# A new hand-written order for the first batch, and the seventh quad's rearrangement moved from GpSimd to VectorE

## The chip, the core and the metric

The kernel runs on one core of a Trainium2 chip. The core has a matrix engine (TensorE, in the profile PE for matmuls and PEld for the loading of their weights), VectorE (DVE), ScalarE (ACT), GpSimd (POOL) and SyncE (SP); 16 DMA engines move data between the chip's main memory and the core's on-chip memory. TensorE writes into PSUM, a small memory of eight banks, from which ScalarE and VectorE read. The metric is the device time in microseconds (us), taken as a median of several runs; lower is better.

## The reference

Attention with a squared ReLU in place of a softmax, and behind it a two-layer network over all heads of a token:

```
scores = (q @ k.T) / sqrt(64)              # per batch and head
attn   = max(scores, 0) ** 2 / 448
x      = (attn @ v), heads side by side    # 3584 x 768
h      = x @ w_in                          # 768 -> 2048
g      = max(h, 0) + alpha * min(h, 0)
out    = g @ w_out                         # 2048 -> 768, float32
```

There are 8 batches, 12 heads, 448 positions and a head width of 64. q, k, v and both weights arrive as float32; the kernel computes in bf16 and sums in float32.

## The kernel before, in words

**Quads and chunks.** Four heads make a quad, three quads a batch, so there are 24 quads. A quad's q and k come as one tile each (`raw`, three buffers per name), v as another (`vraw`, seven buffers). The 448 positions are cut into seven chunks.

**Turning.** Scores need q and k with the head width on the partitions (`T`, four buffers). Quads 0 to 4 are turned by TensorE (`turn_pe`, L149): 28 transposes into PSUM, and copies to `T` by VectorE or ScalarE at L159. From quad 5 on, one engine rearranges the rows into `perm` (L164) and a transposing DMA on SP's queue writes `T` (`turn_dma`, L167).

**Scores.** For each chunk `sc` issues four matmuls (L182) into a pair of PSUM banks, then a Relu by ScalarE (L191) or VectorE (L193) into `rl` (seven buffers). `sq` later squares it, on VectorE (L201) or ScalarE (L199), into `at` (twelve buffers). `late` is the list of chunks that wait for their square; `sq(k)` takes the first k of it.

**A@V.** `attnv` (L204) multiplies a quad's seven squared chunks with v: 28 matmuls (L211) into one pair of banks, which go to `xT`, one half by ScalarE (L221) and one by VectorE (L222); quad 0 alone is copied whole by ScalarE (L219).

**The network.** For the first layer `f1` computes one of 16 slices of 128 columns for a batch: six matmuls (L245), a scaled Relu by ScalarE (L253), and a multiply-add by VectorE (L254). The six matmuls take two from each quad of the batch, so part of a slice can be done before all quads are there: `some_early` does the first four of a slice and holds a PSUM bank for it. `f2` is the second layer, 16 matmuls a tile (L270), a copy by ScalarE (L272) and output DMAs on SP (L278). Columns 0 to 255 of the output use `w_out[0]`, the rest `w_out[1]`.

**Order.** The schedule is manual: each engine executes its instructions in the order in which the program emits them. Loads with a cast are issued from GpSimd's queue, also in order. PSUM banks go to the caller that comes next, always the bank or pair that was taken longest ago. So the order of the lines L286 to L340, the opening for batch 0, fixes four queues at once. Quad 0's q and k are loaded as float32 from SP's and ScalarE's queues and cast on the chip (L138 to L140); a tail of k comes through GpSimd.

**Quad 6.** L382 lets GpSimd rearrange its rows; L394 sends the transposing DMA after the second-layer tile `f2(0, 2, 0)`. The one-element copy to `landed` (L395) makes GpSimd's queue wait until that DMA has landed; behind it lie the last three pieces of `w_out[1]`, q and k of quad 9, and v of quads 6 and 7 (L396 to L399).

Of the kernel before, what the change touches and what calls it, by code (L numbers as in the profile page):

```python
# [16 lines left out]
NJ = 7  # L17
# [3 lines left out]
def kernel(  # L21
# [10 lines left out]
    nc = tc.nc  # L32
    B, H, S, D = q.shape
# [29 lines left out]
    landed = singles.tile([1, 1], BF16)  # L63
# [11 lines left out]
    def take_pair():  # L75
        lo = min((0, 2, 4, 6), key=lambda i: (max(taken[i], taken[i + 1]), i))
        take(lo, 2)
        return psum[:, lo:lo + 2]
# [7 lines left out]
    def take_bank():  # L86
        i = min(range(8), key=lambda i: (taken[i], i))
        take(i, 1)
        return psum[:, i]


    raw, vraw = {}, {}

    def load_qk(n, names="qk"):
        b, g = divmod(n, NG)
        for name in names:
            src = q if name == "q" else k
            t = raw_pool.tile([128, 2, NJ, D], BF16, tag=name, name=f"{name}raw")
            flat = src[b].rearrange("(m two) (pp j) d -> (two pp) m (j d)", two=2, j=NJ)
            nc.gpsimd.dma_start(out=t.rearrange("p m j d -> p m (j d)"), in_=flat[:, 2 * g:2 * g + 2])  # L100
            raw[(n, name)] = t

    def load_v(n):
        b, g = divmod(n, NG)
        t = v_pool.tile([128, 2, NJ, D], BF16, tag="v", name="vraw")
        flat = v[b].rearrange("(m two) (pp j) d -> (two pp) m (j d)", two=2, j=NJ)
        nc.gpsimd.dma_start(out=t.rearrange("p m j d -> p m (j d)"), in_=flat[:, 2 * g:2 * g + 2])  # L107
        vraw[n] = t
# [4 lines left out]
    def load_w_in(i):  # L113
        lo, hi = 512 * i, 512 * i + 512
        for hf in range(2):
            for e in range(2):
                nc.gpsimd.dma_start(out=w_in_sb[64 * hf:64 * hf + 64, :, e, lo:hi],  # L117
                                    in_=w_in_v[hf, e, :, :, lo:hi])

    def load_w_out(h, lo=0, hi=KF, step=4):  # L120
        for lo in range(lo, hi, step):
            nc.gpsimd.dma_start(out=w_out_sb[h][:, lo:lo + step], in_=w_out_v[:, lo:lo + step, COLS[h][0]:COLS[h][1]])

    FIRST = 4
    first, flat0 = {}, {}
# [9 lines left out]
    warm = psum[:, 7, :128]  # L135
    for _ in range(36):
        nc.tensor.matmul(warm, ident, ident, start=True, stop=True)
    for name, lo, hi, copy in (("q", 0, 4, nc.vector.tensor_copy), ("q", 4, NJ, nc.scalar.copy),  # L138
                               ("k", 0, 2, nc.vector.tensor_copy), ("k", 2, FIRST, nc.scalar.copy)):
        copy(raw[(0, name)][:, :, lo:hi].rearrange("p m j d -> p m (j d)"), first[name][:, :, D * lo:D * hi])  # L140
    load_qk(1)
    load_v(0)
    load_qk(2)
# [3 lines left out]
    T = {}  # L147

    def turn_pe(n, parts=(("q", 0, NJ, "D"), ("k", 0, NJ, "D"))):  # L149
        if n not in T:  # L150
            T[n] = T_pool.tile([128, 2, NJ, 128], BF16, tag="T", name="T")
        for name, lo, hi, eng in parts:
            ps = take_bank().bitcast(BF16)
            for j in range(lo, hi):
                for s in range(2):
                    nc.tensor.transpose(ps[64 * s:64 * s + 64, 128 * j:128 * j + 128], raw[(n, name)][:, s, j], ident)  # L156
            dst = T[n][:, "qk".index(name), lo:hi].rearrange("p j c -> p (j c)")
            copy = nc.vector.tensor_copy if eng == "D" else nc.scalar.copy
            copy(dst, ps[:, 128 * lo:128 * hi])  # L159

    def rearrange_rows(n, eng):
        p = perm_pool.tile([128, 2, NJ, 2, D], BF16, tag="perm", name="perm")
        for i, name in enumerate("qk"):
            eng.tensor_copy(p[:, i], raw.pop((n, name)).rearrange("p s j d -> p j s d"))  # L164
        return p

    def turn_dma(n, p=None):  # L167
        p = p or rearrange_rows(n, nc.vector)
        t = T_pool.tile([128, 2, NJ, 128], BF16, tag="T", name="T")
        nc.sync.dma_start_transpose(out=t.rearrange("p a j c -> p (a j) c"),  # L170
                                    in_=p.rearrange("p a j s d -> p (a j s d)"))
        T[n] = t
# [23 lines left out]
    def square(n, j, rl, eng="D"):  # L196
        a = at_pool.tile([128, 2, S], BF16, tag="at", name="at")
        if eng == "A":
            nc.scalar.activation(a, rl, ACTF.Square)  # L199
        else:  # L200
            nc.vector.tensor_tensor(a, rl, rl, ALU.mult)  # L201
        att[(n, j)] = a

    def attnv(n):  # L204
        ps = take_pair()
        vv = vraw.pop(n)
        for j in range(NJ):
            a = att.pop((n, j))
            for r in range(2):
                for s in range(2):  # L210
                    nc.tensor.matmul(ps[64 * s:64 * s + 64, r, :S],  # L211
                                     vv[64 * r:64 * r + 64, s, j, :],
                                     a[64 * r:64 * r + 64, s],
                                     start=(j == 0), stop=(j == NJ - 1))
        b, g = divmod(n, NG)
        if g == 0:
            xT[b] = xT_pool.tile([128, NG, 2, S], BF16, tag="xT", name="xT")
        if n == 0:
            nc.scalar.activation(xT[b][:, g], ps[:, :, :S], ACTF.Copy, scale=out_scale)  # L219
            return  # L220
        nc.scalar.activation(xT[b][:, g, 0], ps[:, 0, :S], ACTF.Copy, scale=out_scale)  # L221
        nc.vector.tensor_scalar(xT[b][:, g, 1], ps[:, 1, :S], out_scale, None, ALU.mult)  # L222

    late = []

    def sc(chunks):

        for n, j, eng in chunks:
            late.append((n, j, relu(score_mm(n, j), eng)))

    def sq(k=99, eng="D"):
        for g in late[:k]:
            square(*g, eng)
        del late[:k]
# [48 lines left out]
    def ch(n, lo, hi, p=pat):  # L283
        return [(n, j, p[j]) for j in range(lo, hi)]

    load_w_in(0)  # L286
    load_v(2)
    load_w_in(1)
    turn_pe(0, (("q", 0, 4, "D"), ("q", 4, NJ, "A"), ("k", 0, 2, "D"), ("k", 2, FIRST, "D")))
    sc(ch(0, 0, 3))  # L290
    turn_pe(0, (("k", FIRST, NJ, "D"),))
    sc(ch(0, 3, 4))
    sq(3)
    load_qk(3)
    sc(ch(0, 4, 6))
    turn_pe(1)
    sc(ch(0, 6, 7))
    sq(4)
    load_w_in(2)
    load_w_in(3)  # L300
    sc(ch(1, 0, 3, "AAA"))
    attnv(0)
    load_qk(4)
    sq(2)
    sc(ch(1, 3, 4))
    turn_pe(2)
    sq(1)
    sc([(1, 4, "D"), (1, 5, "A"), (1, 6, "A")])
    sq(2)
    load_w_out(0, 0, 8)  # L310
    load_qk(5)
    load_v(3)
    load_w_out(0, 8)
    early = {}
    todo = []

    def some_early(count):
        for ff, km in todo[:count]:
            if ff not in early:
                early[ff] = hold()  # L320
            f1_mm(psum[:, early[ff], :S], 0, ff, (km,))
        del todo[:count]

    sc(ch(2, 0, 3, "AAA"))
    sq(3)
    attnv(1)
    load_v(4)
    load_v(5)
    todo = [(ff, km) for ff in range(4) for km in range(4)]
    sc(ch(2, 3, 5, "AAAAAAA"))  # L330
    sq(2)
    some_early(4)
    sc(ch(2, 5, 7, "AAAAADA"))
    some_early(8)
    square(*late.pop(-2), "A")
    sq()
    attnv(2)
    nc.vector.tensor_scalar(beta_sb, alpha_sb, -1.0, 1.0, ALU.mult, ALU.add)
    some_early(4)
    for ff in range(4):  # L340
        f1_mm(psum[:, early[ff], :S], 0, ff, range(4, KM))
        f1_out(psum[:, early[ff], :S], 0, ff)
# [14 lines left out]
            turn_dma(n)  # L357
        load(n + 2)

    turn_pe(3)  # L360
    f1s(0, 4, 6)
    sc(ch(3, 0, 3))
    f1s(0, 6, 8)
# [15 lines left out]
    load_qk(6)  # L379
    load_qk(7)  # L380
    load_qk(8)
    rows6 = rearrange_rows(6, nc.gpsimd)  # L382
    load_w_out(1, 0, 4)
    f2(0, 0, 0)
    sq()
# [5 lines left out]
    sq()  # L391
    f2(0, 1, 0)
    f2(0, 2, 0)
    turn_dma(6, rows6)  # L394
    nc.gpsimd.tensor_copy(landed, T[6][:1, 0, 0, :1])  # L395
    load_w_out(1, 4)  # L396
    load_qk(9)
    load_v(6)
    load_v(7)  # L399
    sc(ch(5, 0, 3))  # L400
    sq(1)
    attnv(4)
# [20 lines left out]
    for ff in range(5):  # L423
        early.append(hold())
        f1_mm(psum[:, early[ff], :S], 1, ff, range(4))
        if ff == 1:
            sc(ch(5, 5, 7))
            sq(1)
            sq(1, "A")
        if ff == 3:  # L430
            attnv(5)
    for ff in range(KF):
        if ff < 5:
            f1_mm(psum[:, early[ff], :S], 1, ff, range(4, KM))
            f1_out(psum[:, early[ff], :S], 1, ff)
            take(early[ff], 1)
        else:
            f1(1, ff)
        if ff in (1, 10):
            turn_dma(7 + ff // 9)  # L440
        if ff == 10:
            nc.gpsimd.tensor_copy(landed, T[8][:1, 0, 0, :1])
            load_v(8)
            load_v(9)
            load(10)
# [21 lines left out]
    for b in range(2, B):  # L467
# [15 lines left out]
        for i, u in enumerate(units):  # L483
            if i in at and not last:
                g = at[i]
# [37 lines left out]
```

## Time and profile before

| what | value |
|---|---|
| median of 4 runs | 386.14 us (386.07 to 386.58) |
| the profiled execution's own time | 386.15 us |
| its span in the profile | 384.2 us |
| TensorE busy | 374.8 us, 3179 matmuls |
| VectorE busy | 265.6 us |
| ScalarE busy | 206.6 us |
| granted TensorE clock | full speed in every slice of the span |
| DMA engines | mean busy share 0.8 or more in each of the first twelve of forty slices |

The span runs from the first to the last instruction; about 2 us of the profiled time lie around it. A line of the timeline reads: start, time from the first instruction's start to the last one's end, engine, line of the code, operation, what is written and read, how many instructions are merged; in brackets the idle time ahead of them and who ended it. Instructions of one engine overlap a little, so the pace of a series is the distance between two starts, and is shorter than one instruction's own time.

### The profile page before, as it was taken

The page shows a single profiled execution, that of the slowest core. Times are in us where ns is not written, and L with a number is a line of the kernel's source. Part 1 is how long each engine was busy: PE and PEld are TensorE (multiplying, and loading weights), DVE is VectorE, ACT ScalarE, POOL GpSimd, SP SyncE. Part 2 cuts the span into 40 slices and gives each one's busy share as a digit, 9 for nine tenths or more (in the row PEclk, how much of TensorE's full clock was granted, in tenths as well). Part 3 has the DMA queues.
Part 4 walks back from the last instruction along what each step waited for, and adds up shares of the span by engine and source line. Part 5 has one row for each costly group of instructions (what it writes and reads, how often), then busy time and mean ns, then how long its engine had stood idle before and what let it go on. Part 6 is the DMA issues. An engine that isn't in the chain of part 4 may idle for free.

```text
span 384.2 us, 7843 instructions
## 1 busy us (share of the span) xinstructions
PE 374.8 (98%) x3179; PEld 205.7 (54%) x3200; DVE 265.6 (69%) x420; ACT 206.6 (54%) x331; POOL 70.1 (18%) x106
## 2 busy tenths in 40 slices
PE   7799999999999999999999999999999999999996
PEld 6444565555544455545465555544556445645554
DVE  4987987777657988688656887779855788526300
ACT  5978687445643654465444656547544475434321
POOL 8557070507302202022200222020000000000000
PEclk9999999999999999999999999999999999999999
DMA  9999989999993766687292872946035300120023
GB/s 161 190 202 202 189 125 196 171 175 207 220 220 61 109 116 109 109 134 119 49 165 60 135 122 51 166 77 119 15 85 88 77 0 15 44 68 2 14 68 85
DMA packets 73284, 43.42 MB, mean 113 GB/s; under 512 B 40352, under 2 KB 69792, under 8 KB 73248
## 3 DMA queue, kind: packets, MB, share of 16 engines
q0 software_dynamic: 26864, 22.45, 39.5%
q1 hardware_dynamic: 45952, 20.07, 26.7%
q8 instruction: 25, 0.41, 0.4%
q10 hardware_dynamic: 432, 0.39, 0.3%
q14 instruction: 11, 0.09, 0.1%
HBM read 45.62 MB, written 11.01 MB: 147 GB/s over the span
## 4 chain that ended last, share of the span: by engine, by line
PE 94%; DVE 3%; DMA 1%; issue 0%; ACT 0%; ACTq 0%
PE psum L245 38%; PE psum L270 38%; PE psum L182 9%; PE psum L211 8%; DVE at L201 2%; DMA qfirst<-in_q_dram 1%; PE psum L156 1%; DVE T L159 1%; DVE rl L193 1%; ACT osb L272 0%; DVE xT L222 0%; DVE qraw L140 0%; ACTq L278 0%; ACT T L159 0%
## 5 line engine op out<-in xcount | busy, mean ns | idle before, releaser
L270 PE MATMUL psum<-w_out,gT 128*128 128x256 bf16 (+3 forms) x891 | 149.9, 322 | 1.1
L245 PE MATMUL psum<-xT,w_in_sb 128*128 128x448 bf16 x768 | 150.1, 353 | 0.1
L270 PEld LDWEIGHTS <-gT 128*128 128x128 bf16 x912 | 86.7, 98 | 64.2 <-issue 8.2
L245 PEld LDWEIGHTS <-w_in_sb 128*128 128x128 bf16 x768 | 73.5, 98 | 73.2 <-issue 6.2
L254 DVE SCALAR_TENSOR_TENSOR gT<-neg,beta_sb,psum 128x448 bf16<-128x448 f32 x128 | 83.6, 678 | 35.4 <-ACT neg L253 35.3
L253 ACT ACTIVATE neg<-psum 128x448 f32<-128x448 f32 x128 | 69.2, 546 | 61.2 <-PE psum L245 59.4
L191 ACT ACTIVATE rl<-psum 128x896 bf16<-128x896 f32 x113 | 97.9, 931 | 1.7 <-PE psum L182 1.7
L201 DVE TENSOR_TENSOR at<-rl 128x896 bf16<-128x896 bf16 x164 | 92.1, 621 | 0.0
L193 DVE TENSOR_SCALAR rl<-psum 128x896 bf16<-128x896 f32 x55 | 59.7, 1086 | 40.3 <-PE psum L182 40.1
L272 ACT COPY osb<-psum 128x256 f32<-128x256 f32 (+3 forms) x57 | 26.9, 473 | 104.7 <-PE psum L270 99.0
L182 PE MATMUL psum<-T 64*64 64x448 bf16 x672 | 44.9, 356 | 3.0 <-DVE T L159 1.1
L100 POOL DMA_DIRECT2D qraw<-in_q_dram x23 | 16.6, 724 | 137.5 <-DVE perm L164 135.5
L211 PE MATMUL psum<-at,vraw 64*64 64x448 bf16 x672 | 36.7, 350 | 0.3 <-DVE at L201 0.2
L182 PEld LDWEIGHTS <-T 64*64 64x64 bf16 x672 | 16.7, 106 | 21.4 <-issue 13.1
L211 PEld LDWEIGHTS <-vraw 64*64 64x64 bf16 x672 | 21.1, 106 | 12.6 <-issue 2.5
L222 DVE TENSOR_SCALAR xT<-psum 128x448 bf16<-128x448 f32 x23 | 14.4, 624 | 14.4 <-PE psum L211 10.3
L107 POOL DMA_DIRECT2D vraw<-in_v_dram x24 | 17.5, 732 | 2.9 <-PE psum L182 1.0
L100 POOL DMA_DIRECT2D kraw<-in_k_dram x23 | 16.7, 727 | 2.5 <-DVE at L201 0.8
L221 ACT ACTIVATE xT<-psum 128x448 bf16<-128x448 f32 x23 | 12.6, 550 | 2.6 <-PE psum L211 2.6
L117 POOL DMA_DIRECT2D w_in_sb<-in_moe_w_in_dram x16 | 10.0, 632 | 6.3 <-DMA vraw<-in_v_dram 1.9
L164 DVE COPY perm<-kraw 128x896 bf16<-128x896 bf16 x18 | 11.0, 611 | 0.1
L164 DVE COPY perm<-qraw 128x896 bf16<-128x896 bf16 x18 | 11.0, 614 | 0.0
(29 smaller groups left out, 43.0 us busy)
## 6 DMA issues: line engine op xcount, KB each, us to landing
out_dram<-osb SPq DMA_DIRECT2D x54, 128.0 KB, 2.4
vraw<-in_v_dram POOLq DMA_DIRECT2D x24, 224.0 KB, 8.0
qraw<-in_q_dram POOLq DMA_DIRECT2D x23, 224.0 KB, 5.4
kraw<-in_k_dram POOLq DMA_DIRECT2D x23, 224.0 KB, 7.3
out_dram<-osb SPq DMA_DIRECT2D x56, 64.0 KB, 2.2
w_in_sb<-in_moe_w_in_dram POOLq DMA_DIRECT2D x16, 192.0 KB, 8.5
w_out<-in_moe_w_out_dram POOLq DMA_DIRECT2D x4, 512.0 KB, 9.2
w_out<-in_moe_w_out_dram POOLq DMA_DIRECT2D x4, 256.0 KB, 8.7
```

Source lines behind the costliest of these rows:

```text
L100: nc.gpsimd.dma_start(out=t.rearrange("p m j d -> p m (j d)"), in_=flat[:, 2 * g:2 * g + 2])
L164: eng.tensor_copy(p[:, i], raw.pop((n, name)).rearrange("p s j d -> p j s d"))
L182: nc.tensor.matmul(ps[64 * c:64 * c + 64, r, :S], t[64 * r:64 * r + 64, 1, j, 64 * c:64 * c + 64], t[64 * r:64 * r + 64, 0, :, 64 * c:64 * ...
L191: nc.scalar.activation(rl, ps[:, :, :S], ACTF.Relu)
L193: nc.vector.tensor_scalar(rl, ps[:, :, :S], 0.0, None, ALU.max)
L201: nc.vector.tensor_tensor(a, rl, rl, ALU.mult)
L211: nc.tensor.matmul(ps[64 * s:64 * s + 64, r, :S], vv[64 * r:64 * r + 64, s, j, :], a[64 * r:64 * r + 64, s], start=(j == 0), stop=(j == NJ ...
L245: nc.tensor.matmul(ps, w_in_sb[:, km // 2, km % 2, bass.ts(ff, 128)], xT[b][:, km // 2, km % 2, :], start=(km == 0), stop=(km == KM - 1))
L253: nc.scalar.activation(neg, ps, ACTF.Relu, scale=-1.0)
L254: nc.vector.scalar_tensor_tensor(gT[b // 2][:, ff, (b % 2) * S:(b % 2) * S + S], neg, beta_sb[:, ff:ff + 1], ps, ALU.mult, ALU.add)
L270: nc.tensor.matmul(ps, gT[sb][:, ff, bass.ts(c, 128)], w_out_sb[h][:, ff, lo:hi], start=(ff == 0), stop=(ff == KF - 1))
L272: nc.scalar.copy(o[:, lo:hi], ps)
```

## The change

- Quad 0: the casts are cut into six pieces (`cast0`), q on both engines and k on ScalarE alone; the turning is cut into nine pieces with a PSUM bank each.
- The order of batch 0 is written out anew: which chunk's Relu, which square, which copy comes when on which engine. `sq_of` squares a named chunk. The first two A@V come after the third quad's second chunk, and the 16 early matmuls of the first layer are issued as 11 and 5, all ahead of A@V of quad 2.
- Quad 0's A@V result is copied in halves by two engines, like the others'.
- In GpSimd's queue q and k of quad 3 come ahead of the second piece of `w_in`, and q and k of quad 4 ahead of its fourth.
- Quad 3 is turned ahead of the end of the first four slices, not behind them.
- Quad 6 is rearranged by VectorE inside `turn_dma(6)`, which now comes behind A@V of quad 5; the `landed` copy and the loads that were behind it move along.

```diff
-    for name, lo, hi, copy in (("q", 0, 4, nc.vector.tensor_copy), ("q", 4, NJ, nc.scalar.copy),
-                               ("k", 0, 2, nc.vector.tensor_copy), ("k", 2, FIRST, nc.scalar.copy)):
-        copy(raw[(0, name)][:, :, lo:hi].rearrange("p m j d -> p m (j d)"), first[name][:, :, D * lo:D * hi])
...
-        if n == 0:
+        if eng == "A":
             nc.scalar.activation(xT[b][:, g], ps[:, :, :S], ACTF.Copy, scale=out_scale)
...
+    def sq_of(n, j, eng):
+        for g in [g for g in late if g[:2] == (n, j)]:
+            square(*g, eng)
+            late.remove(g)
+
+    def cast0(name, lo, hi, eng):
+        copy = nc.vector.tensor_copy if eng == "D" else nc.scalar.copy
+        copy(raw[(0, name)][:, :, lo:hi].rearrange("p m j d -> p m (j d)"), first[name][:, :, D * lo:D * hi])
+
+    load_w_in(0)
+    load_v(2)
+    cast0("q", 4, 6, "A")
+    cast0("q", 0, 2, "D")
+    cast0("q", 6, 7, "A")
+    cast0("q", 2, 4, "D")
+    cast0("k", 0, 2, "A")
+    cast0("k", 2, 4, "A")
+    turn_pe(0, (("q", 0, 2, "D"),))
+    turn_pe(0, (("q", 4, 6, "A"),))
+    turn_pe(0, (("q", 2, 4, "D"),))
+    turn_pe(0, (("q", 6, 7, "A"),))
+    turn_pe(0, (("k", 0, 1, "D"),))
+    turn_pe(0, (("k", 1, 2, "A"),))
+    turn_pe(0, (("k", 3, 4, "A"),))
+    turn_pe(0, (("k", 2, 3, "A"),))
+    sc([(0, 0, "A")])
+    sc([(0, 1, "D")])
+    turn_pe(0, (("k", 4, 7, "D"),))
+    load_qk(3)
+    load_w_in(1)
+    load_w_in(2)
+    sq_of(0, 0, "D")
+    sc([(0, 2, "A")])
+    sc([(0, 3, "A")])
+    sq_of(0, 1, "D")
+    turn_pe(1, (("q", 0, 7, "D"),))
+    sc([(0, 4, "A")])
+    sc([(0, 5, "A")])
+    turn_pe(1, (("k", 0, 7, "D"),))
+    load_qk(4)
+    load_w_in(3)
+    sq_of(0, 2, "D")
+    sq_of(0, 5, "D")
+    sc([(0, 6, "A")])
+    sq_of(0, 4, "D")
+    sq_of(0, 6, "D")
+    sc([(1, 0, "A")])
+    sq_of(0, 3, "D")
+    sc([(1, 1, "A")])
+    sc([(1, 2, "D")])
+    sc([(1, 3, "A")])
+    sc([(1, 4, "A")])
+    sq_of(1, 0, "D")
+    turn_pe(2, (("k", 0, 5, "D"),))
+    turn_pe(2, (("q", 0, 7, "D"),))
+    sq_of(1, 2, "D")
+    sq_of(1, 4, "D")
+    turn_pe(2, (("k", 5, 7, "A"),))
...
+    sc([(1, 5, "A")])
+    sc([(1, 6, "A")])
+    sc([(2, 0, "A")])
+    sc([(2, 1, "A")])
+    sq_of(1, 1, "D")
+    sq_of(1, 5, "D")
+    sq_of(1, 3, "D")
+    sq_of(1, 6, "D")
+    attnv(0, "AD")
+    sc([(2, 2, "A")])
+    attnv(1, "AD")
+    sc([(2, 3, "A")])
+    sc([(2, 4, "D")])
+    sq_of(2, 0, "A")
+    some_early(11)
+    sq_of(2, 4, "A")
+    sc([(2, 5, "A")])
+    sq_of(2, 1, "D")
+    sq_of(2, 3, "D")
+    sq_of(2, 2, "D")
+    sc([(2, 6, "D")])
+    sq_of(2, 5, "A")
+    some_early(5)
+    sq_of(2, 6, "D")
     nc.vector.tensor_scalar(beta_sb, alpha_sb, -1.0, 1.0, ALU.mult, ALU.add)
-    some_early(4)
+    attnv(2, "AD")
+    some_early(0)
+    turn_pe(3, (("q", 0, 7, "D"),))
+    turn_pe(3, (("k", 0, 7, "D"),))
     for ff in range(4):
         f1_mm(psum[:, early[ff], :S], 0, ff, range(4, KM))
...
-    turn_pe(3)
     f1s(0, 4, 6)
...
-    rows6 = rearrange_rows(6, nc.gpsimd)
     load_w_out(1, 0, 4)
...
     f2(0, 2, 0)
-    turn_dma(6, rows6)
-    nc.gpsimd.tensor_copy(landed, T[6][:1, 0, 0, :1])
-    load_w_out(1, 4)
-    load_qk(9)
-    load_v(6)
-    load_v(7)
     sc(ch(5, 0, 3))
...
         if ff == 3:
             attnv(5)
+            turn_dma(6)
+            nc.gpsimd.tensor_copy(landed, T[6][:1, 0, 0, :1])
+            load_w_out(1, 4)
+            load_qk(9)
+            load_v(6)
+            load_v(7)
```

## The prediction, made before the changed kernel was built or run

> **What bounds the kernel now.** First the page's busy times and the chain that ended last:
>
> ```profile
> PE 374.8 (98%) x3179; PEld 205.7 (54%) x3200; DVE 265.6 (69%) x420; ACT 206.6 (54%) x331; POOL 70.1 (18%) x106
> ...
> PE 94%; DVE 3%; DMA 1%; issue 0%; ACT 0%; ACTq 0%
> ```
>
> TensorE sets the end. The change takes no matmul away, so it can only give back time in which TensorE waits. The stages (after each stage's length: PE, PEld, DVE, ACT, POOL busy, with counts) show where:
>
> ```profile
> 5.45:20.15 14.70, 11.48 (x217) 6.57 (x217) 13.78 (x27) 13.82 (x19) 9.08 (x15) 1.00 1.24 189
> 20.15:28.05 7.90, 7.90 (x92) 3.93 (x88) 6.31 (x12) 6.08 (x10) 4.79 (x8) 1.00 1.25 203
> 28.05:384.20 356.15, 351.42 (x2843) 191.39 (x2860) 244.92 (x382) 184.85 (x301) 51.51 (x74) 1.00 0.63 107
> ```
>
> From 5.45 to 20.15 both ScalarE and VectorE are busy for nearly 13.8 of 14.7 us: the opening is bound by Relus, squares and copies, not by TensorE. (Of the 4.7 idle in the last row, nearly 4 are the tail behind the last matmul, at 380.6.) Then the timelines of ScalarE, VectorE and TensorE:
>
> ```profile
> 7.03 7.40 ACT L191 ACTIVATE rl<-psum 128x896 bf16<-128x896 f32 x9 [0.48 <-PE psum L182]
> 14.22 1.02 ACT L219 ACTIVATE xT<-psum 128x896 bf16<-128x896 f32 x1
> 15.02 5.08 ACT L191 ACTIVATE rl<-psum 128x896 bf16<-128x896 f32 x6
> 19.86 0.67 ACT L221 ACTIVATE xT<-psum 128x448 bf16<-128x448 f32 x1
> 20.30 2.66 ACT L191 ACTIVATE rl<-psum 128x896 bf16<-128x896 f32 x3
> ```
>
> ```profile
> 11.16 3.30 DVE L201 TENSOR_TENSOR at<-rl 128x896 bf16<-128x896 bf16 x6
> ```
>
> ```profile
> 20.15 0.98 PE L245 MATMUL psum<-xT,w_in_sb 128*128 128x448 bf16 x4
> 21.05 0.72 PE L182 MATMUL psum<-T 64*64 64x448 bf16 x8
> 21.71 1.69 PE L245 MATMUL psum<-xT,w_in_sb 128*128 128x448 bf16 x8
> 23.33 1.52 PE L211 MATMUL psum<-at,vraw 64*64 64x448 bf16 x28
> 24.78 2.44 PE L245 MATMUL psum<-xT,w_in_sb 128*128 128x448 bf16 x12
> ```
>
> ScalarE has no idle time from 7.03 on. TensorE catches up at 20.15, with the first early product, and reaches slice 4 of the first layer at 28.06. One more wait lies behind it:
>
> ```profile
> 54.64 0.91 DVE L201 TENSOR_TENSOR at<-rl 128x896 bf16<-128x896 bf16 x1
> 55.47 0.61 DVE L222 TENSOR_SCALAR xT<-psum 128x448 bf16<-128x448 f32 x1
> ```
>
> ```profile
> 54.07 0.98 POOL L164 COPY perm<-qraw 128x896 bf16<-128x896 bf16 x1
> ```
>
> ```profile
> 55.33 1.91 PE L245 MATMUL psum<-xT,w_in_sb 128*128 128x448 bf16 x8
> ```
>
> A square takes 0.91 beside GpSimd's rearranging copy, where it takes 0.62 elsewhere; VectorE's half of A@V of quad 4 starts late, ends at 56.08, and TensorE's fourth product waits: 1.91 for eight matmuls that take 1.69 at 21.71.
>
> **Paces**, start to start: Relu on ScalarE 0.80 ((14.22-7.03)/9); square on VectorE 0.54 ((3.30-0.62)/5), Relu there 1.00 (21.55 to 22.55), a full turn copy 0.54; half of A@V 0.44 on ScalarE (19.86 to 20.30), 0.55 on VectorE (19.90 to 20.45); first-layer matmul 0.19; A@V of a quad 1.35; 28 transposes 0.90 (27.15 to 28.06); a change of matmul kind about 0.1.
>
> **The start: nothing.** Today the first Relu starts at 7.03, behind ScalarE's copy of the last q chunks (6.07 to 6.55). In the new order ScalarE has four casts and five turn copies ahead of it. The trace has casts of 256 and 384 columns in 0.41 and 0.51, turn copies of 384 and 896 in 0.48 and 0.91; so 128 columns cost 0.30 and 0.27, each 0.1 less where the next follows. Casts from 4.84 to 6.01, q 4 and 5 copied by 6.29, q 6 ends at 6.56, matmuls at 6.61, Relu at 7.04; the three copies of k fit in by 6.97. [...]
>
> **The opening, queue by queue.** ScalarE from 7.04: ten Relus (and 0.1 for an `rl` buffer whose square, chunk 3 of quad 0, now comes late, 13.46) to 15.10; the last piece of quad 2's turn 0.28; four Relus to 18.57; half of A@V 0 to 19.01; Relu of quad 2's chunk 2 to 19.81 (its bank is free at 19.93); half of A@V 1, done at 20.36. VectorE from 7.22: two Relus 2.0, turn copies 0.26, 1.07 and 0.94, fourteen squares 7.5, waits 0.1: quad 1's last square ends at 19.16, today 19.93. Fourteen squares now lie ahead of A@V of quad 0 with twelve `at` buffers, so the thirteenth (18.0) waits for that A@V, which runs from 16.4: 1.5 to spare. A@V 1 gives its result at 19.63, VectorE's half is done at 20.26.
>
> TensorE: the first early product at 19.98, eleven of them to 22.1, two chunks to 22.6, five products to 23.6. A@V of quad 2 must wait for a pair of banks, since four banks are held: for the Relu of chunk 5, which ScalarE reaches behind the Relu of chunk 3 (20.25) and two squares (0.85 each, from two in 1.79 at 50.45): 22.75 to 23.67. So A@V 23.72 to 25.1, turning of quad 3 to 26.0, the eight last products to 27.55: slice 4 comes 0.5 sooner than 28.06. The gain is mostly not speed: the second half of the early products is done in one run, with fewer changes of kind, and covers what was waiting.
>
> Bounds: with TensorE never waiting from 19.98 on, 0.65 sooner. With squares on ScalarE at 1.10 (the one at 22.69) Relu 5 ends 0.5 later and nothing is gained. The pace of two in series is the nearer row; I take -0.45.
>
> Does data keep up? Quad 3's q and k change places with the second piece of `w_in`: v of quad 2 lands at 19.72, six transfers later it is 26.01 in both orders (DMA share over 1.2 throughout). So quad 3 is there by 22, for 25.1, and slice 4's weights by 26.0, for 27.55: 1.5 to spare. Quad 4's k landed at 36.53 and is turned at 36.64; a TensorE 0.5 ahead would have waited for it. Loaded before the last piece of `w_in` it lands about 33, and that piece at about 36.5 instead of 34.75, used from 39.9. Worth nothing by itself, but without it the gain would be lost there.
>
> **Quad 6 off GpSimd: -0.2.** The square at 54.64 returns to 0.62, TensorE's eight products to 1.69. The two copies cost VectorE 1.08 (0.61 each, 0.53 start to start) behind A@V of quad 5, at 61.5; there it idles 1.15 today until ScalarE's scaled Relu, 62.67. Were that cover gone, the multiply-adds would come 1.1 later, with three free banks, 3 us of matmuls, before TensorE would feel it: nothing.
>
> SP now issues the transposing DMA at about 62.6, not 57.28, with no output waiting behind it; quad 7's follows, today at 65.06. It landed at 67.32. Those of quads 5 and 7 took 5.95 and 5.63: so 68.2 to 68.6, and GpSimd's loads go out 1 us later. Quad 7's may now meet those loads; even at the 14.9 that quad 8's took beside them (72.79 to 87.67) it lands by 81, for 87.5. The last piece of `w_out[1]` landed at 81.2 (issued 69.4, 11.8) and is first used by the 13th matmul of the tile that starts at 81.0, at 83.8; new: 82.2 against 83.1. v of quad 6 lands at about 86.8, for 90.4. k of quad 9 lands at 85.2; VectorE waits 1 us for it, ahead of an idle 3.7. All hidden.
>
> **Sum:** 386.15 - 0.45 - 0.2 = 385.5, and the same against the median, 386.14.
>
> **Rivals.**
> A (45%): as above, 385.5, between 385.3 and 385.7.
> B (25%): TensorE runs without a wait from 19.9, and ScalarE's queue is a little ahead of my walk: 0.65 and 0.22, and 0.1 to 0.2 from the start; 385.1. For it: the walk adds every handshake. Against: two engines are full, and ScalarE has more to do in the new opening than before (two more squares, 1.7, less one Relu and half of a copy).
> [...]
> D (10%), slower: the transposing DMA of quad 6 gates the second weights. It may land 1.9 later than today, 69.2, before the 13th matmul above waits (2.6 of slack, less 0.7 by which TensorE is ahead); each us beyond is a us of the end. At the 10.0 that it took in this trace it would land at 72.6: 3.4 lost, 388.9. Against it: what delayed it then, the loads of quads 6 to 8, has landed by 63.14.
>
> **Numbers.** 385.5. Low 385.0 (B's end); high 386.3 (all of C); D's 10% is left out, and little below. Within 0.2% (0.77 us, about what can be told from no change): most of A and all of C, 0.57; faster by more: B and a little of A, 0.33; slower: D, 0.10.
>
> **What would show it.** First Relu at 7.0; early products from 20.0, in runs of eleven and five; A@V of quad 2 at 23.7 behind a Relu of ScalarE; slice 4 at 27.5. No square of 0.91 near 54. The `landed` copy near 68.5, and no gap in TensorE at 80 to 84. Wrong if TensorE waits in the first 20 us for a piece of `T` or a bank that I have free, if slice 4 waits for weights, or if a step of the tile at 81 is missing its weights.

## The result, and the profile after

The changed kernel takes 385.61 us (median of 35 executions, 385.44 to 387.38); the kernel before took 386.3 (median of 55, 385.79 to 387.31). The ratio of the mean times is 0.9989, 95% interval 0.9984 to 0.9994. The profiled execution took 385.47, with a span of 383.7, and its last matmul starts at 379.80 instead of 380.41, 0.61 sooner.

The executions of the changed kernel fall into two groups, and the median and the ratio can't be understood without them: 20 of 35 lie at 385.44 to 385.62 with a mean granted clock of 0.999 or 1, and 15 at 386.18 to 387.38 with 0.996 or less. The kernel before has one group, around 386.3; in the 89 executions of it beside the experiments the clock is never under 0.998. The first lines below are of the first group; the second group has its own experiments.

TensorE's busy time and the chain have the same shape as before:

```profile
PE 374.9 (98%) x3179; PEld 206.1 (54%) x3200; DVE 266.1 (69%) x422; ACT 208.3 (54%) x339; POOL 68.3 (18%) x104
...
PE 95%; DVE 2%; DMA 1%; ACT 1%; issue 0%; ACTq 0%; DVEq 0%
```

The stages, cut where they were cut before:

```profile
5.45:20.15 14.70, 12.12 (x217) 6.97 (x216) 13.49 (x27) 14.70 (x27) 8.91 (x14) 1.00 1.25 189
20.15:28.05 7.90, 7.90 (x90) 4.04 (x90) 6.94 (x13) 6.33 (x10) 5.21 (x8) 1.00 1.24 204
28.05:383.70 355.65, 350.87 (x2838) 191.23 (x2857) 245.12 (x383) 185.42 (x303) 49.46 (x72) 1.00 0.64 108
```

In the first stage ScalarE (fourth pair) is now busy for all of the 14.70, and TensorE (first pair) for 12.12 where it was for 11.48. ScalarE's timeline, then TensorE's:

```profile
5.99 1.03 ACT L156 COPY T<-psum 128x256 bf16<-128x256 bf16 x5
7.00 8.21 ACT L184 ACTIVATE rl<-psum 128x896 bf16<-128x896 f32 x10
...
19.65 0.75 ACT L214 ACTIVATE xT<-psum 128x448 bf16<-128x448 f32 x1
20.07 1.14 ACT L184 ACTIVATE rl<-psum 128x896 bf16<-128x896 f32 x1
20.87 2.00 ACT L192 ACTIVATE at<-rl 128x896 bf16<-128x896 bf16 x2
22.68 1.00 ACT L184 ACTIVATE rl<-psum 128x896 bf16<-128x896 f32 x1
```

```profile
20.02 2.30 PE L238 MATMUL psum<-xT,w_in_sb 128*128 128x448 bf16 x11
22.25 0.57 PE L175 MATMUL psum<-T 64*64 64x448 bf16 x8
22.75 1.12 PE L238 MATMUL psum<-xT,w_in_sb 128*128 128x448 bf16 x5
23.80 1.52 PE L204 MATMUL psum<-at,vraw 64*64 64x448 bf16 x28
25.25 0.58 PE L153 MATMUL psum<-ident,qraw 128*64 128x128 bf16 x14
25.66 0.56 PE L153 MATMUL psum<-ident,kraw 128*64 128x128 bf16 x14
26.15 2.63 PE L238 MATMUL psum<-xT,w_in_sb 128*128 128x448 bf16 x13
```

The first Relu is at 7.00, the first early product at 20.02, the runs are eleven and five, and A@V of quad 2 starts at 23.80 right behind ScalarE's Relu of 22.68. The last row starts with the eight products that complete the first four slices, 0.19 each; slice 4 starts behind them, at 27.68, 0.38 sooner than 28.06. Around 54, VectorE's timeline and then TensorE's:

```profile
54.25 0.61 DVE L194 TENSOR_TENSOR at<-rl 128x896 bf16<-128x896 bf16 x1
54.79 0.62 DVE L215 TENSOR_SCALAR xT<-psum 128x448 bf16<-128x448 f32 x1
```

```profile
54.95 1.69 PE L238 MATMUL psum<-xT,w_in_sb 128*128 128x448 bf16 x8
```

The square takes 0.61 and the eight products 1.69. From start to the next start they took 1.84 before (55.33 to 57.17) and take 1.61 now (54.95 to 56.56): 0.22 before rounding. So 0.38 + 0.22 = 0.60 of the 0.61. Behind the rearranging the transposing DMA of quad 6 is issued at 62.02, and GpSimd's wait for it ends here:

```profile
66.61 0.18 POOL L467 COPY landed<-T 1x1 bf16<-1x1 bf16 x1 [11.66 <-DMA T<-perm]
```

It had ended at 67.44 in the kernel before. The whole list of what TensorE waited for (line, cause, us in total, times, longest) has no weights in it:

```profile
PE psum L137 <- POOL ident masks.py:199: 1.4, 1, 1.4
PE psum L175 <- ACT rl L184: 1.0, 4, 0.4
PE psum L175 <- DVE T L156: 0.9, 2, 0.6
PE psum L153 <- DMA kraw<-in_k_dram: 0.5, 1, 0.5
```

The last row is new: k of quad 2 landed at 13.62, before at 12.42. It delays nothing that follows at 20: in old_start below, k landed at 12.74, there is no such wait, and slice 4 comes just as long behind the first Relu (20.68).

### The profile page after: what moved, and what is told of

It reads as the page before. It is cut to its first block, busy times and chain, and to the rows that moved or that the text cites. A ratio compares the mean times of both kernels' runs of the same rounds, so it can differ in the third digit from the quotient of the medians.

```text
span 383.7 us, 7855 instructions
## 1 busy us (share of the span) xinstructions
PE 374.9 (98%) x3179; PEld 206.1 (54%) x3200; DVE 266.1 (69%) x422; ACT 208.3 (54%) x339; POOL 68.3 (18%) x104
## 4 chain that ended last, share of the span: by engine, by line
PE 95%; DVE 2%; DMA 1%; ACT 1%; issue 0%; ACTq 0%; DVEq 0%
PE psum L238 38%; PE psum L263 38%; PE psum L175 9%; PE psum L204 8%; DVE at L194 1%; DMA qfirst<-in_q_dram 1%; DVE T L156 1%; DVE rl L186 0%; PE psum L153 0%; ACT osb L265 0%; ACT kraw L296 0%; ACT qraw L296 0%; ACTq L271 0%; ACT T L156 0%; DVEq L186 0%
## 5 line engine op out<-in xcount | busy, mean ns | idle before, releaser
L194 DVE TENSOR_TENSOR at<-rl 128x896 bf16<-128x896 bf16 x162 | 90.6, 619 | 0.0
L186 DVE TENSOR_SCALAR rl<-psum 128x896 bf16<-128x896 f32 x56 | 60.8, 1086 | 40.5 <-PE psum L175 40.3
L214 ACT ACTIVATE xT<-psum 128x448 bf16<-128x448 f32 x24 | 13.4, 560 | 2.3 <-PE psum L204 2.3
```

Source lines behind the costliest of these rows:

```text
L186: nc.vector.tensor_scalar(rl, ps[:, :, :S], 0.0, None, ALU.max)
```

## The experiments

Each had eleven executions, one of them profiled (quad4_late twelve, vector_old_place five). "At full clock" are those with a mean granted clock of 0.998 or more. Ratios are to the kernel before, run beside each. The first four rows come from one chip, the next four from another, the last three from a third, on which the kernel before took 386.30, 386.34 and 386.26; differences of less than 0.1 between rows of different chips are not read. "Changed" is the changed kernel, 385.47 at full clock, last matmul at 379.80. Edits are to it unless the text says otherwise.

| run | median us | ratio (95%) | at full clock: number, median | slice 4 in the profile | last matmul |
|---|---|---|---|---|---|
| gpsimd_back | 385.99 | 0.9994 (0.9985 to 1.0002) | 9 of 11, 385.98 | 27.68 | 380.29 |
| quad6_alone | 386.00 | 0.9992 (0.9983 to 1.0000) | 11 of 11, 386.00 | 28.05 | 380.17 |
| old_start | 385.68 | 0.9993 (0.9983 to 1.0003) | 6 of 11, 385.54 | 27.86 | 379.97 |
| quad4_late | 385.80 | 0.9993 (0.9982 to 1.0005) | 8 of 12, 385.58 | 28.53, low clock | 380.65 |
| five_behind | 386.50 | 1.0011 (1.0000 to 1.0022) | 8 of 11, 386.50 | 28.69 | 380.81 |
| turn3_behind | 386.40 | 1.0009 (1.0000 to 1.0018) | 6 of 11, 386.37 | 29.40, low clock | 381.53 |
| vector_old_place | 397.88 | 1.0295 (1.0268 to 1.0321) | 0 of 5 | – | – |
| products_sooner | 385.69 | 0.9988 (0.9979 to 0.9997) | 7 of 11, 385.64 | 28.00 | 380.12 |
| two_more | 385.59 | 0.9982 (0.9973 to 0.9991) | 11 of 11, 385.59 | 28.11 | 380.22 |
| one_more | 385.59 | 0.9979 (0.9970 to 0.9988) | 11 of 11, 385.59 | 27.82 | 379.94 |
| changed_again | 385.51 | 0.9982 (0.9973 to 0.9992) | 8 of 11, 385.49 | 28.61, low clock | 380.72 |

Intervals of 0.001 don't tell the first four from each other; there the traces decide.

### Quad 6 back on GpSimd, and quad 6 alone

```diff
+    rows6 = rearrange_rows(6, nc.gpsimd)
     load_w_out(1, 0, 4)
...
     f2(0, 2, 0)
+    turn_dma(6, rows6)
...
-            turn_dma(6)
```

> The changed kernel with quad 6 rearranged by GpSimd again and its transposing DMA and loads at their old place. Theory (two gains that add up: about 0.4 in the opening, 0.2 from the GpSimd copy that no longer blocks a square): slice 4 of the first layer starts at 27.66 as in the changed kernel, a square near 54 takes 0.9 again, the eight products behind it 1.84 instead of 1.61, and the end comes 0.2 later, so -0.3 to -0.4 against before. Rival (all of the gain is in the opening, the GpSimd copy hurts nobody who sets the end): the last matmul starts where it does in the changed kernel, 379.8. Rival (the whole gain is quad 6): no better than before.

For the other run the edit is made to the kernel before, and is this part of the change alone (the rearrangement at its new place, with `landed` and the loads).

> The kernel before with only quad 6 moved: VectorE rearranges it behind A@V of quad 5, the transposing DMA and the loads behind it move along. Theory: slice 4 at 28.06 as before, the square at 0.62, the last matmul at 380.2 instead of 380.4, -0.2 against before. Rival (the later transposing DMA delays the second weights): TensorE waits between 80 and 84, no gain or a loss.

VectorE's timeline with GpSimd back, then GpSimd's and TensorE's:

```profile
54.25 1.18 DVE L198 TENSOR_TENSOR at<-rl 128x896 bf16<-128x896 bf16 x1
```

```profile
54.00 0.94 POOL L161 COPY perm<-qraw 128x896 bf16<-128x896 bf16 x1
```

```profile
54.95 0.74 PE L242 MATMUL psum<-xT,w_in_sb 128*128 128x448 bf16 x3
56.02 1.11 PE L242 MATMUL psum<-xT,w_in_sb 128*128 128x448 bf16 x5 [0.34 <-DVE xT L219]
57.06 0.57 PE L179 MATMUL psum<-T 64*64 64x448 bf16 x8
```

The square that starts at 54.25 takes 0.61 in the changed kernel and 1.18 here, because GpSimd's copy runs from 54.00 to 54.94; TensorE then waits for VectorE's half. The copy costs 0.50 here (54.95 to 57.06 in place of 1.61), more than the 0.2 expected and than the 0.22 that the kernel before paid: the square started 0.57 behind the copy's start there (54.64 against 54.07), 0.25 behind it here, so 0.41 of it lay under the copy then and 0.69 now. It grew by 0.30 and by 0.57, which is 0.73 and 0.83 of those times: it nearly stands while the copy runs. Slice 4 is untouched, at 27.68. Alone, the move gives 0.24 in the last matmul (380.17 against 380.41), as expected, and 0.3 in the median. So the two parts are separate, and "the whole gain is quad 6" falls, as does "the GpSimd copy hurts nobody who sets the end".

### The old start

```diff
-    cast0("q", 4, 6, "A")
...
-    turn_pe(0, (("k", 2, 3, "A"),))
+    cast0("q", 0, 4, "D")
+    cast0("q", 4, NJ, "A")
+    cast0("k", 0, 2, "D")
+    cast0("k", 2, FIRST, "A")
+    turn_pe(0, (("q", 0, 4, "D"), ("q", 4, NJ, "A"), ("k", 0, 2, "D"), ("k", 2, FIRST, "D")))
```

> The changed kernel with quad 0 cast in four pieces, turned in five and copied as before (q 0 to 3 and k 0 to 1 cast by VectorE, the rest by ScalarE), all else of the new order kept. Theory (the pieces are worth nothing): first Relu at 7.0, slice 4 within 0.1 of 27.66, time as the changed kernel. Rival (the finer start is the gain): slice 4 at about 28.0, the opening's 0.4 is gone.

At full clock it is 385.54 against 385.47. In its profile the first Relu comes at 7.18 instead of 7.00, but the first cast starts 0.09 later too (q landed later), and the clock opens at 5.80 instead of 5.04 (the first 14 transposes take 0.73 there, from 5.44, and 0.58 in the changed kernel, from 5.32). From the Relu on nothing differs: slice 4 follows 20.68 behind it, exactly as in the changed kernel (27.68 - 7.00). Two profiles with a like opening of the clock show what the start itself is worth: 7.03 with the old one (before, opened at 5.34), 6.99 with the new one (five_behind, at 5.37). So the finer start is not the gain, and the pieces are worth little in either direction, under 0.1.

### Quad 4 loaded late

```diff
-    load_qk(4)
     load_w_in(3)
+    load_qk(4)
```

> The changed kernel with q and k of quad 4 loaded behind the last piece of w_in. Prediction as written: k lands at about 36.4, TensorE wants to turn quad 4 from 36.18 and waits, so that up to all of the opening's 0.4 is lost there. Weaker form: the 14 transposes of k come 0.45 behind those of q, at 36.6, so TensorE waits 0.1 or not at all, and the load order is worth nothing. Slice 4 at 27.66 in both.

385.58 at full clock, and TensorE's waits hold no row for quad 4's q or k. Its profiled execution had a low clock and was itself 0.85 late, which would hide a wait of up to that size; but k landed at 36.33 in it, and the changed kernel starts to turn k at 36.59. Eight executions at full clock show no loss of 0.4 either. The sentence "without it the gain would be lost there" is not borne out. It took the start of quad 4's turning for that of k: q is turned first, and k's transposes started at 36.98 in the kernel before, 0.45 behind the landing at 36.53.

### What in the order makes the gain

Five products behind A@V of quad 2:

```diff
-    some_early(5)
...
     attnv(2, "AD")
-    some_early(0)
+    some_early(5)
```

> The changed kernel with the last five of the sixteen early products moved behind A@V of quad 2. Theory (A@V of quad 2 can't start before ScalarE's Relu of chunk 5 frees a pair of banks at 23.68, and the five products fill that wait): A@V still starts at about 23.75, TensorE idles about 0.9 ahead of it, slice 4 comes 0.9 to 1.0 later, +0.9 against the changed kernel. Rival (TensorE is simply full): A@V starts 0.9 sooner and the time is unchanged.

Quad 3 turned behind the first four slices, in place of ahead of their ends:

```diff
-    turn_pe(3, (("q", 0, 7, "D"),))
-    turn_pe(3, (("k", 0, 7, "D"),))
     for ff in range(4):
         f1_mm(psum[:, early[ff], :S], 0, ff, range(4, KM))
...
+    turn_pe(3, (("q", 0, 7, "D"),))
+    turn_pe(3, (("k", 0, 7, "D"),))
```

> The changed kernel with quad 3 turned behind the first four slices, as before the change. Theory (turning covers the copy of A@V of quad 2, which in the kernel before was covered by four early products): the eight last products start at about 26.15 as now, behind VectorE's half at 26.09, TensorE idles 0.8 ahead of them, and the turning comes on top: slice 4 at 28.5, +0.85 against the changed kernel. Rival (the order of the two is indifferent): unchanged.

One new row in each list of TensorE's waits, the first kernel's and then the second's:

```profile
PE psum L204 <- ACT rl L184: 0.9, 1, 0.9
```

```profile
PE psum L238 <- ACT xT L214: 0.6, 1, 0.6
```

Both come out as expected: 1.0 and 0.9 later at full clock, which is more than the opening's whole gain, so each ends level with the kernel before or just above it. (The 29.40 of turn3_behind's profile holds a stretch at low clock too, and is not used.) A@V of quad 2 starts at 23.80 with the five products ahead of it and at 23.73 with them behind it: work put ahead of it is nearly free, work put behind it is not.

Products still sooner, as 4, 4, 3 and 5, with a single chunk between:

```diff
-    todo = [(ff, km) for ff in range(4) for km in range(4)]
+    todo = [(ff, km) for two in ((0, 1), (2, 3)) for ks in ((0, 1), (2, 3)) for ff in two for km in ks]
...
+    some_early(4)
+    sq_of(2, 1, "D")
     sc([(2, 4, "D")])
     sq_of(2, 0, "A")
-    some_early(11)
-    sq_of(2, 4, "A")
+    some_early(4)
     sc([(2, 5, "A")])
-    sq_of(2, 1, "D")
+    some_early(3)
+    sq_of(2, 4, "A")
```

> The changed kernel with the early products started ahead of chunk 4 of quad 2, in an order that takes those of quad 0 first, and chunk 5's matmuls ahead of the last eight. Theory (the opening is at its floor: ScalarE's and VectorE's squares end at 24.6, and A@V of quad 2 ends behind them): first product at 19.7 instead of 20.02, slice 4 at most 0.15 sooner, time unchanged within what can be told. Rival (TensorE's start of the products is what counts): slice 4 0.3 sooner.

```profile
19.74 0.93 PE L238 MATMUL psum<-xT,w_in_sb 128*128 128x448 bf16 x4
20.60 0.38 PE L175 MATMUL psum<-T 64*64 64x448 bf16 x4
20.91 0.93 PE L238 MATMUL psum<-xT,w_in_sb 128*128 128x448 bf16 x4
21.77 0.38 PE L175 MATMUL psum<-T 64*64 64x448 bf16 x4
22.09 0.74 PE L238 MATMUL psum<-xT,w_in_sb 128*128 128x448 bf16 x3
22.76 0.38 PE L175 MATMUL psum<-T 64*64 64x448 bf16 x4
23.08 1.12 PE L238 MATMUL psum<-xT,w_in_sb 128*128 128x448 bf16 x5
24.12 1.52 PE L204 MATMUL psum<-at,vraw 64*64 64x448 bf16 x28
```

Both expectations miss: the first product is 0.28 sooner, at 19.74, and slice 4 is 0.32 later, at 28.00. TensorE has no idle time in these rows; the same work takes longer. From the first product to A@V of quad 2 there are 4.38 (19.74 to 24.12), in the changed kernel 3.78 (20.02 to 23.80). One chunk more lies in it here, 0.25 at the pace of two in one piece (0.50, from 22.25 to 22.75 above). What is left, 0.35, goes with four more changes of the kind of matmul; that would be about 0.09 each, an estimate that no run tried alone.

### VectorE at GpSimd's old place

Edit to the kernel before:

```diff
-    rows6 = rearrange_rows(6, nc.gpsimd)
+    rows6 = rearrange_rows(6, nc.vector)
```

> The kernel before with quad 6 rearranged by VectorE at the place where GpSimd did it. Theory (not the engine but the place makes the move free): the copies stand in VectorE's queue ahead of the squares and Relus of quad 4 and 5 and wait for q of quad 6 at 53.5 and k at about 56, so A@V of quad 3 or 4 waits for squares or Relus, and TensorE loses 3 us or more; slower by about 1%. Rival (VectorE has room there): as before or 0.2 faster.

TensorE's waits, VectorE's timeline, and the stages around it (length, busy times with counts, clock, DMA share, GB/s):

```profile
PE psum L182 <- DVE rl L193: 11.2, 2, 10.5
```

```profile
54.25 0.62 DVE L164 COPY perm<-qraw 128x896 bf16<-128x896 bf16 x1 [7.69 <-DMA qraw<-in_q_dram]
57.02 0.62 DVE L164 COPY perm<-kraw 128x896 bf16<-128x896 bf16 x1 [2.15 <-DMA kraw<-in_k_dram]
```

```profile
49.20:52.70 3.50, 0.02 (x4) 0.00 (x0) 0.00 (x0) 2.17 (x3) 2.26 (x4) 1.00 0.37 67
52.80:62.90 10.10, 3.14 (x17) 1.96 (x17) 6.34 (x10) 0.95 (x1) 2.85 (x4) 0.50 1.17 175
```

11.5 us slower; "3 us or more" was expected, so the direction was right and the size far off. The copies cost 0.62 each; what costs is their place. VectorE meets the first one 7.69 before q of quad 6 has landed, and all that is queued behind it, Relus that TensorE needs a bank from, stands too. So the change's gain of 0.22 needs the engine and the place together. The two stages show a second loss: TensorE stood still for the 3.50 of the first, and its clock was at half for all 10.10 of the second.

### The second group: where the clock goes

In the profiled executions of quad4_late, turn3_behind and changed_again the granted clock falls to 0.50 for 3.41 us, from 13.80, 13.96 and 14.21 on, and opens again. The record shows steps only at multiples of 3.41 from the first opening, and that opening came between 4.45 and 7.39. Cut at each execution's own steps, the rows are, for the changed kernel's first profile, for its second one, and for quad6_alone, which has the old order:

```profile
8.45:11.86 3.41, 2.69 (x52) 1.31 (x49) 3.41 (x8) 3.41 (x6) 1.59 (x4) 1.00 1.26 203
11.86:15.27 3.41, 2.22 (x44) 1.26 (x43) 3.41 (x6) 3.41 (x7) 1.79 (x3) 1.00 1.20 174
15.27:18.68 3.41, 3.10 (x60) 1.99 (x63) 3.41 (x8) 3.41 (x6) 2.07 (x4) 1.00 1.23 191
```

```profile
7.38:10.79 3.41, 3.02 (x58) 1.58 (x54) 3.07 (x6) 3.41 (x5) 1.97 (x4) 1.00 1.23 193
10.79:14.21 3.42, 1.86 (x26) 0.86 (x28) 3.42 (x7) 3.42 (x5) 1.89 (x3) 1.00 1.19 182
14.21:17.62 3.41, 3.41 (x49) 2.17 (x49) 3.41 (x7) 3.11 (x5) 1.88 (x3) 0.50 1.20 186
```

```profile
7.86:11.27 3.41, 2.17 (x44) 1.28 (x43) 3.41 (x8) 3.41 (x6) 2.01 (x3) 1.00 1.26 198
```

Look at PE (first pair) and at the clock (the third number from the end). A window with 1.86 of TensorE busy is followed by one at half clock; 2.22 and 2.17 are not. The profiles of quad4_late and turn3_behind had 1.78 and 1.72 in theirs. In the half-clock window TensorE is busy for all of it with fewer matmuls, 49, where the first profile has 60 between 14.21 and 17.62: here it is on the path. The first early product comes at 20.95 in place of 20.02, and the 0.93 stays to slice 4 (28.61).

Not all of the 0.93 is that window's. ScalarE's first Relu in the same execution:

```profile
7.34 0.92 ACT L184 ACTIVATE rl<-psum 128x896 bf16<-128x896 f32 x1 [0.21 <-PE psum L175]
```

It is 0.34 late already, behind matmuls that ran before the clock opened at 7.38. How slow such matmuls are, quad4_late shows: its first 14 transposes, from 5.32 and ahead of an opening at 6.97, take 0.96, where they take 0.58 in the changed kernel's first profile. From the first Relu to slice 4 it is 21.27 here and 20.68 in the first profile, so the half-clock window costs 0.59; quad4_late's profile gives 0.60 (7.25 to 28.53). All three low profiles opened late, between 6.97 and 7.38, so the second group holds both losses.

The weak stretch lies in the new order. A@V of quad 0, 28 matmuls, lay at 12.05 in the kernel before and lies at 16.34 now; from 10.4 to 13.8 TensorE is busy for 1.86 (25 matmuls) where it was for 2.46 (48). The kernel before, then the changed one:

```profile
10.40:13.80 3.40, 2.46 (x48) 1.38 (x44) 3.40 (x7) 3.40 (x5) 1.98 (x3) 1.00 1.26 193
```

```profile
10.40:13.80 3.40, 1.86 (x25) 0.74 (x26) 3.40 (x7) 3.40 (x5) 1.46 (x2) 1.00 1.27 193
```

In none of these profiles, the three low ones included, was TensorE of the new order out of work for more than 0.73 us at a time there.

So a window without work was not needed: one in which TensorE was busy for 1.72 to 1.86 of 3.41 came ahead of each of the three half-clock windows.

How often? With the first profile's matmuls, a window of 3.41 has less than 2.17 busy when it starts between 9.4 and 10.7, that is for 1.3 of 3.41 possible starts, 39%. This is an estimate: it takes every start as equally likely, and 2.17 for the bound. With the matmuls of the kernel before no start gives less than 2.17. Measured, for the changed kernel: 18 of 46 executions (39%), and none of 89 of the kernel before.

To test it, work was added that TensorE can do in this stretch without delaying anybody: score matmuls of six chunks (quad 0's chunk 6, quad 1's 0 to 4) are issued three times, or twice, into the same bank, each time with the same operands and with `start=True`.

```diff
+    MORE = {(0, 6), (1, 0), (1, 1), (1, 2), (1, 3), (1, 4)}
...
-        for r in range(2):
-            for c in range(2):
-                nc.tensor.matmul(ps[64 * c:64 * c + 64, r, :S],
+        for _ in range(3 if (n, j) in MORE else 1):
+            for r in range(2):
+                for c in range(2):
+                    nc.tensor.matmul(ps[64 * c:64 * c + 64, r, :S],
```

> The changed kernel with the score matmuls of chunk 6 of quad 0 and chunks 0 to 4 of quad 1 issued three times into the same banks (the second and third time write the same values over; nothing is left out). In two profiled variants of the changed kernel the granted clock was at half from 13.8 to 17.2, with TensorE busy 0.52 of the 3.4 us before; in the kernel before the same stretch is busy 0.72 and in none of 62 runs does the mean clock fall under 0.998. Theory (the new order leaves TensorE too idle between 10 and 14, and in some executions, by the phase of the clock's windows, the gate closes for 3.41 us): with the repeats, 0.38 us for a chunk and with 0.5 us in hand ahead of each Relu, no run has a mean clock of 0.996, all runs lie at 385.4 to 385.6, where 20 of 35 runs of the changed kernel lie, and the median is 0.1 to 0.2 lower. Rival (the two groups of runs have another cause, chip or memory): still 3 to 5 of 11 runs at 386.2 and more with a clock of 0.996.

> As e9, each of the six chunks twice: half of the added work, about 1.1 us of matmul time in all. Theory: fewer runs at 386.3 than of the changed kernel (15 of 35), perhaps none; first and second theory differ as in e9.

> The changed kernel as it is, beside e9 and e10 on the same chip, so that its two groups of runs are counted there too. Theory: again two groups, about 4 in 10 runs at 386.2 to 386.4 with a mean clock of 0.996, the others at 385.5.

The window of two_more that starts where the changed kernel's weak one did:

```profile
10.80:14.22 3.42, 3.07 (x64) 1.67 (x60) 3.42 (x7) 3.42 (x5) 2.08 (x3) 1.00 1.24 186
14.22:17.63 3.41, 2.94 (x68) 2.12 (x68) 3.41 (x7) 3.41 (x6) 1.87 (x3) 1.00 1.22 191
```

Its clock opened at 7.39, as the second profile's did at 7.38: with 3.07 in the window in place of 1.86 it stays full. None of the 22 executions with repeats is under 0.998, 3 of 11 of the changed kernel beside them are, at 386.06, 386.26 and 386.42. The windows of the two profiles with repeats hold 2.71 to 3.29 of TensorE busy (two_more from 7.39, one_more from 10.06). So busy matmuls in that stretch hold the clock here, and the rival in the expectation, that the groups come from the chip or the memory, falls. That the repeats make a faster kernel is not shown: the median was expected to be 0.1 to 0.2 lower and is not (385.59 and 385.59 against 385.51), and only the upper group is gone.

At full clock the kernels with repeats lie 0.1 above the changed one (385.59 against 385.49), but that need not be the price of the repeats. Late openings stay in their count, while in the changed kernel, as far as the profiles show, they fall into the second group and leave the count. two_more's profiled execution shows one: first Relu at 7.35, no window at half clock, slice 4 at 28.11, and with 385.88 the slowest of its eleven. From the first Relu to slice 4 it takes 20.76, and one_more takes 20.68 (7.14 to 27.82), where the changed kernel takes 20.68.

## Why the prediction was right, and where not

**The opening, -0.45: right, 0.38.** Each step of the walk came within 0.15: Relu at 7.00 (7.04 predicted), last square of quad 1 ending at 19.10 (19.16), ScalarE's half of A@V of quad 1 done at 20.40 (20.36), first product 20.02 (19.98), A@V of quad 2 at 23.80 (23.72), slice 4 at 27.68 (27.55). The reason, products in fewer pieces and as cover for what was waiting, is borne out by five_behind, turn3_behind and products_sooner: each undoes a part of it and loses. Rival B's 0.65 was not reached, and the one try to get nearer to it, products_sooner, lost 0.32. The bound's price for the squares on ScalarE, 1.10 each or 2.2 for two, was not met: from the first one's start to the next Relu they took 1.81 (20.87 to 22.68), where A took 1.7. Two readings were off without harm: the tail behind the last matmul's end at 380.6 is 3.6 of the 384.2, not nearly 4, and quad 3's k landed at 22.66, not by 22, which still left 3 us.

**Quad 6, -0.2: right.** 0.22 in the products, 0.24 when done alone, and 0.50 when GpSimd's copy is put back at a worse moment.

**The start, nothing: right.** The high end of the range, and the 0.20 of the chances that go with it (C), rest in part on a fixed price for each small piece; no run shows one. In the profile of before a cast of 0.51 starts at 4.84 and the next one at 5.27, and the changed kernel's five turn copies on ScalarE take 1.03 in all, where one of 128 columns takes 0.28: each overlaps its neighbour. The first Relu came at 7.00, VectorE's first, from which its queue was walked, at 7.26 (7.22 before), and old_start puts the pieces at under 0.1.

**Rival D: the term was mis-sized, in the safe direction.** The prediction gave quad 6's transposing DMA 5.6 to 6.0 us and a landing at 68.2 to 68.6. It took 4.47, from 62.02, and `landed` came at 66.61, 0.83 sooner than before. The two neighbours that it was sized by, 5.95 and 5.63, were too few: in the profile of before such transfers take 4.0 to 14.9. With it k of quad 9 landed at 81.53, not at 85.2. No weight was missing at 81.

**Quad 4's load:** worth nothing, as predicted; the sentence on what would be lost without it was wrong, by the start of k's transposes (36.98, not 36.64).

**What it missed: the clock.** The prediction put all idle time of TensorE before 20 at nothing, "the opening is bound by Relus, squares and copies, not by TensorE". For the path that held; for the clock it did not. 18 of 46 executions are about 0.8 longer (386.3 against 385.47), which is as much as the gain; by the traces some 0.6 of it is the half-clock window that the emptier stretch brings, and the rest goes with the late opening. That is why the mean moves by 0.11% only, while at full clock it is 0.83 of 386.3, 0.21%. The median, 385.61, is the upper end of the first group because that group holds 20 of the 35 executions. So the mechanisms were right, but that the median lies 0.1 from the predicted 385.5 is partly luck: with three executions more in the second group it would be near 386.2, still inside the range and almost no gain.

Left open: the exact share of busy time at which the clock falls. It lies between 1.86 and 2.17 of 3.41 in these profiles; with 1.9 for the bound the same estimate gives 12% of the starts, so the measured 39% speaks for the upper end. The number of matmuls alone does not set it: from 345.1 to 348.5 the first profile holds 20 matmuls, fewer than the 24 and 26 of the weak windows of quad4_late and changed_again, but is busy throughout, and the clock stays at 1.00. Open too is why the first group lies 0.83 below the kernel before, where the trace gives 0.61. Part of it may be the choice of executions: at full clock the changed kernel keeps, as far as the profiles show, only those that did not open late, and the 386.3 of before holds all. The profile of before (386.15) also lies under that 386.3. And of the new order, only what lies around A@V of quad 2 and the start was tried alone; what quad 0's A@V in halves, the place of quad 3's load and the order of the other Relus and squares are worth was not.

## What to carry to other kernels

An order is gained where a wait has work in front of it that could also be done behind it: put such work ahead of the wait (five products put behind it cost 1.0 here), in as few runs of a kind as possible (four runs of products in place of two brought slice 4 0.32 later), and walk every queue with the paces of the trace. Moving an operation to another engine is half an edit; its place in that engine's queue, and whether its data has landed by then, is the other half (0.22 gained against 11.5 lost). When work is taken out of a stretch in which TensorE has time to spare, look at TensorE's busy time there over 3.41 us, the length of the half-clock windows in these traces: with 1.72 to 1.86 of it busy, TensorE lost half its clock in a stretch where it was off the path, and paid 0.59 when it was back on it.

## What the runs showed of the hardware

- The granted clock fell to 0.50 for one window of 3.41 us after a window with 1.72 to 1.86 us of matmuls and no pause over 0.73 (quad4_late, turn3_behind, changed_again), and did not after 2.17 (quad6_alone) or 2.22 (the changed kernel's first profile). In the two profiles of the changed kernel the windows start elsewhere (first openings at 5.04 and 7.38), and the weakest of the opening holds 2.22 in one and 1.86 in the other.
- With a late opening of the clock the first Relu came later too: at 7.34 and 7.35 with openings at 7.38 and 7.39 (changed_again, two_more), and at 7.00 with one at 5.04.
- A square on VectorE of 0.61 beside a copy on GpSimd took 0.91 or 1.18, by how much of it lay under the copy (0.41 or 0.69).
- Five copies from PSUM by ScalarE in series took 0.2 each, and cutting the casts and copies of quad 0 from nine pieces into fifteen cost nothing that the times tell (385.47 against 385.54 with the old start).
- The transposing DMA of quad 6 took 4.47 where it had taken 10.04 in the profile of before; there the same form took 4.0 to 14.9 us over all quads.
